# Weights of a fused GLA and gated-MLP kernel: half of each matrix as plain f32 blocks between the input loads, half by casting DMAs, and a new instruction order

## Chip, cores, metric

One core of a Trainium2 chip. The metric is device microseconds of the whole program, lower is better. "Before" and "changed" always mean the two kernels of this document. Spans in a profile are some 2 us shorter than the device time of the same run (192.9 for 195.0).

## The reference, cut to what matters

```python
def _attn_ref(q, k, v, alpha):                 # 4 x 8 heads, 768 steps, head size 48
    for t in range(S):
        state = alpha[:, :, t, :, None] * state + einsum('bhd,bhe->bhde', k[:, :, t], v[:, :, t])
        y[:, :, t] = einsum('bhd,bhde->bhe', q[:, :, t], state)

def _moe_ref(x, w_in, w_out):                  # x: 3072 x 384, w_in: 384 x 2048, w_out: 2048 x 384
    h = x @ w_in
    return (h * cos(h)) @ w_out
```

The kernel cuts the time steps into 24 chunks of 128 and computes each with matmuls; two chunks make a group for the MLP.

## The kernel before

It is a list of small units, emitted in the order of one long string. Each engine runs its own units strictly in that order, so the string is five in-order queues braided into one. A letter is a kind of unit, the number a chunk, a group or a piece:

```python
units = {
    "a": load_a, "k": load(k_t, k), "q": load(q_t, q), "v": load(v_t, v), "w": load_w,    # SyncE; w: GpSimd
    ...                                          # i l c C d E: Ln, cumulative sums, Exp
    "K": scale_k, "R": lambda j: scale_q(nc.gpsimd, j), "O": lambda j: scale_q(nc.vector, j),
    "P": cast_v, "M": decay,                     # GpSimd
    "T": transposes, "t": ev_transposes, "D": dma_transposes,   # TensorE + VectorE, or one DMA on SyncE
    "S": state, "u": ev_state, "b": ...,         # state, TensorE, VectorE, GpSimd
    "A": scores, "m": mask_scores, ... "Q": outputs_two, "z": ev_outputs_two,
    "F"/"H": first product, "f"/"h": cosine on ScalarE, "p"/"g": gate on VectorE,
    "V": second, "e": ev_second, "o": store, "x": warmup,       # o: SyncE
}
for u in ORDER.split():
    units[u[0]](int(u[1:]))
```

(comments and the joined F/H lines are mine, "..." marks cuts). The loads concerned:

```python
def load(bufs, src):
    return lambda j: nc.sync.dma_start(out=bufs[j % len(bufs)], in_=rows(src, j))   # 192 KB in rows of 192 B

def load_w(i):                                   # f32 in memory, bf16 in SBUF: the DMA casts
    n = NF // 2
    if i < 2:
        f = slice(i * n * C, (i + 1) * n * C)
        nc.gpsimd.dma_start(out=w1[:, :, f], in_=moe_w_in[:, f].rearrange("(k p) f -> p k f", p=C))
    else:
        ...                                      # w_out, half i - 2
```

All inputs, the stores and the DMA transposes of chunks 8 to 23 share SyncE's queue; chunks 0 to 7 are transposed on TensorE.

## Time and profile before

| | before |
|---|---|
| time | 195.33 us median of 3 (195.08 to 195.69); with a fourth run 195.26, as below |
| TensorE busy | 182.5 us of 192.9 (95%), 17.1 of it warm-up matmuls |
| VectorE, ScalarE, GpSimd busy | 61%, 62%, 42% |
| HBM read, written | 25.17 MB, 4.72 MB |

How to read the lines below: a row of the windows view gives a stretch, its length, the busy time of each engine with its instruction count, the granted TensorE clock (1.00 is full), the DMA share and GB/s. In a timeline or chain a line starts with its start and its length in us; brackets give the idle time of the engine just before and what ended it. A waits line gives total, number and longest. The lines that carry the reading of the kernel before stand in the prediction.

```profile
44.00:85.00 41.00, 40.84 (x484) 30.86 (x483) 26.86 (x30) 29.02 (x34) 24.63 (x37) 1.00 1.19 199
85.00:160.00 75.00, 73.12 (x806) 54.66 (x804) 48.92 (x49) 60.63 (x65) 36.72 (x56) 1.00 1.06 188
```

### The profile page before, as it was taken

To read this page: it belongs to the slowest core of one execution; us is meant where nothing else is said; L and a number is where in the kernel's file an instruction comes from. 1 tells how busy PE (TensorE), PEld (TensorE's weight loads), DVE (VectorE), ACT (ScalarE), POOL (GpSimd) and SP (SyncE) were. 2 spreads that over 40 slices of the span, in tenths; PEclk is the share of its full clock that TensorE was granted. 3 is DMA by queue.
4 is the path that set the end of the run, shared out by engine and by line. 5 is a ranking of instruction groups with operands and counts; after the bars stand their busy time and mean duration, and the time that the engine had idled before them with its cause. 6 is when DMAs were issued, how large, how long until landed. Compare 5 with 4: busy or idle time off the path is not lost.

```text
span 192.9 us, 4781 instructions
## 1 busy us (share of the span) xinstructions
PE 182.5 (95%) x1990; PEld 131.8 (68%) x1994; DVE 117.7 (61%) x138; ACT 120.1 (62%) x133; POOL 81.6 (42%) x128
## 2 busy tenths in 40 slices
PE   7997889989999999997999998999999999999993
PEld 2444468957688687685777685786786786876861
DVE  5025784844847928829828438748758578596450
ACT  2540344744768668947739567789999982361632
POOL 3317950055294655571190656271239761030000
PEclk9999999999999999999999999999999999999999
DMA  6999999999989999999989999999998762200112
GB/s 127 188 187 188 146 190 188 184 196 194 190 192 176 205 233 207 188 168 196 268 162 192 175 214 218 175 227 205 149 217 158 135 152 34 85 0 3 41 41 82
DMA packets 123092, 31.23 MB, mean 162 GB/s; under 512 B 117184, under 2 KB 122304, under 8 KB 123072
## 3 DMA queue, kind: packets, MB, share of 16 engines
q1 hardware_dynamic: 120192, 27.80, 85.0%
q0 software_dynamic: 2880, 3.15, 10.1%
q8 instruction: 15, 0.25, 0.5%
q14 instruction: 5, 0.04, 0.1%
HBM read 25.17 MB, written 4.72 MB: 155 GB/s over the span
## 4 chain that ended last, share of the span: by engine, by line
PE 66%; DMA 13%; SPq 6%; ACT 4%; issue 4%; DVE 3%; POOL 2%; ACTq 0%; DVEq 0%
PE one L362 31%; PE two L341 21%; DMA w<-in_moe_w_out_dram 10%; PE two L303 6%; SPq L158 5%; PE two L243 3%; DVE g_sb L352 3%; DMA v_sb<-in_v_dram 2%; ACT c_sb L347 2%; PE two L191 2%; SPq L161 2%; ACT L347 1%; PE one L257 1%; POOL w L167 1%; PE two L193 1%
## 5 line engine op out<-in xcount | busy, mean ns | idle before, releaser
L352 DVE TENSOR_TENSOR g_sb<-two,c_sb 128x1024 bf16<-128x1024 f32 x48 | 58.0, 1221 | 27.7 <-ACT c_sb L347 27.2
L362 PE MATMUL one<-w,g_sb 128*128 128x384 bf16 x384 | 69.5, 327 | 1.4 <-DVE g_sb L352 0.8
L341 PE MATMUL two<-xT,w 128*128 128x256 bf16 (+1 forms) x624 | 68.4, 264 | 1.0 <-DVE g_sb L352 1.0
L347 ACT ACTIVATE c_sb<-two,halfpi 128x1024 bf16<-128x1024 f32 x48 | 52.6, 1113 | 19.5 <-PE two L341 19.0
L341 PEld LDWEIGHTS <-w 128*128 128x128 bf16 x624 | 56.7, 98 | 9.7 <-issue 1.1
L362 PEld LDWEIGHTS <-g_sb 128*128 128x128 bf16 x384 | 35.3, 98 | 24.0 <-DVE g_sb L352 1.7
L206 POOL TENSOR_TENSOR kqb<-k_sb,icp 128x384 bf16<-128x384 f32 x24 | 23.9, 997 | 20.5 <-DMA k_sb<-in_k_dram 12.6
L262 POOL TENSOR_TENSOR ub<-sc,Em 128x384 bf16<-128x384 f32 x20 | 16.6, 829 | 33.1 <-DVE sc L272 31.8
L248 DVE TENSOR_TENSOR A_sb<-two,mask_f 128x1024 bf16<-128x1024 f32 x24 | 28.5, 1217 | 2.6 <-PE two L243 2.6
L212 POOL TENSOR_TENSOR kqb<-q_sb,cp 128x384 bf16<-128x384 f32 x22 | 21.9, 998 | 9.4 <-DMA q_sb<-in_q_dram 5.7
L366 ACT ACTIVATE o_sb<-one 128x384 f32<-128x384 f32 x24 | 11.7, 492 | 15.5 <-PE one L362 15.5
L347 ACT ACT_TABLE_LOAD x11 | 14.1, 1283 | 9.9 <-PE two L341 6.2
L216 POOL CAST vpb<-v_sb 128x384 bf16<-128x384 f32 x24 | 12.0, 504 | 17.2 <-DMA v_sb<-in_v_dram 9.3
L375 PE MATMUL one<-warm 128*128 128x512 bf16 x62 | 17.1, 418 | 2.2 <-DVE warm L102 1.2
L185 ACT ACTIVATE lnab<-a_sb 128x768 bf16<-128x768 f32 (+1 forms) x13 | 10.3, 794 | 12.5 <-DMA a_sb<-in_alpha_dram 12.4
L201 ACT ACTIVATE icp<-two 128x768 f32<-128x768 f32 (+1 forms) x13 | 9.9, 761 | 11.8 <-PE two L193 9.0
L272 DVE TENSOR_TENSOR sc<-one,ub 128x384 f32<-128x384 f32 x20 | 11.0, 552 | 8.2 <-PE one L257 7.9
L321 DVE CAST xT<-two 128x768 bf16<-128x768 f32 x11 | 10.5, 958 | 8.4 <-PE two L303 8.4
L179 ACT ACT_TABLE_LOAD x11 | 14.1, 1283 | 0.9 <-PEq L404 0.7
L303 PE MATMUL two<-A_sb,vpb 128*64 128x128 bf16 x264 | 13.2, 220 | 0.1
L303 PEld LDWEIGHTS <-vpb 128*64 128x64 bf16 x288 | 12.8, 110 | 0.5 <-issue 0.3
L375 PEld LDWEIGHTS <-warm 128*128 128x128 bf16 x66 | 6.4, 104 | 9.6 <-issue 3.6
(42 smaller groups left out, 114.1 us busy)
## 6 DMA issues: line engine op xcount, KB each, us to landing
k_sb<-in_k_dram SPq DMA_DIRECT2D x24, 192.0 KB, 4.6
a_sb<-in_alpha_dram SPq DMA_DIRECT2D x24, 192.0 KB, 4.3
v_sb<-in_v_dram SPq DMA_DIRECT2D x24, 192.0 KB, 4.4
q_sb<-in_q_dram SPq DMA_DIRECT2D x24, 192.0 KB, 4.2
out_dram<-o_sb SPq DMA_DIRECT2D x24, 192.0 KB, 3.7
w<-in_moe_w_in_dram POOLq DMA_DIRECT2D x2, 768.0 KB, 10.0
w<-in_moe_w_out_dram POOLq DMA_DIRECT2D x2, 768.0 KB, 17.7
qkT<-kqb SPq DMA_TRANSPOSE x16, 3.8
```

Source lines behind the costliest of these rows:

```text
L179: nc.scalar.preload_act_table_set("natural_log_exp_and_others")
L206: nc.gpsimd.tensor_tensor(out=kqb[j % 4][:, 0, :, 0:D], in0=k_t[j % 6], in1=icp_t[j // 2 % 3][:, j % 2].rearrange("s (h d) -> s h d", h=H) ...
L212: eng.tensor_tensor(out=kqb[j % 4][:, 1, :, 0:D], in0=q_t[j % 6], in1=cp.rearrange("s (h d) -> s h d", h=H), op=ALU.mult)
L216: nc.gpsimd.tensor_copy(out=vpb[j % 4][:, :, 0:D], in_=v_t[j % 6])
L248: nc.vector.tensor_tensor(out=A_t[j % 4].rearrange("s (h t) -> s h t", h=H), in0=two[("A", j)].rearrange("s (h t) -> s h t", h=H), in1=mas ...
L262: eng.tensor_tensor(out=ub[j % 3][:, :, 0:96].rearrange("r p (a e) -> r p a e", a=2), in0=src.rearrange("r p (a e) -> r p a e", a=2), in1= ...
L303: nc.tensor.matmul(t[64 * half : 64 * half + 64, kt * C : (kt + 1) * C], lhsT, rhs, start=start, stop=stop, skip_group_check=True)
L341: nc.tensor.matmul(t[:, m * n : (m + 1) * n], w1[:, kk, f * C : (f + 1) * C], x_t[g % 3][:, kk, bs].rearrange("r b t -> r (b t)"), start=( ...
L347: nc.scalar.activation(out=c_s.take((name, i)), in_=two[(name, i)], func=AF.Sin, bias=halfpi, scale=1.0)
L352: nc.vector.tensor_tensor(out=g_t[g % 3][:, fs, bs], in0=shaped(two[(name, i)], name), in1=shaped(c_s[(name, i)], name), op=ALU.mult)
L362: nc.tensor.matmul(one[("o", j)][:, 0:DM], g_t[j // 2 % 3][:, f, j % 2], w2[:, f], start=(f == 0), stop=(f == NF - 1))
L375: nc.tensor.matmul((one.free or two.free)[0][:, 0:512], warm[:, 0:C], warm, start=True, stop=True)
```

## The change

The intent: the MLP can start only when weights are there, and the casting loads come late and in one lump. So the first halves of both matrices come as seven plain f32 blocks (three of w_in with 4 KB rows, four of w_out) between the first input loads, are cast by whichever engine has time, and only the second halves are cast by DMA. The order is new throughout: DMA transposes already for chunks 5 to 7, seven k products and six more q products on VectorE instead of GpSimd, fewer warm-ups. Cut to its core:

```diff
 ORDER = """
-k1 a0 a3 a1 k0 v1 q0 a2 q2 i0 x12 c0 v3 d0 k2 M0 i1 x7 c1 k3 K0 d1 q1 K1 q3 P1 O0 x13 T0 v0 l1 t0
+a1 W1 k1 a0 q0 i1 i0 W0 q1 x20 c0 c1 k0 v0 d1 d0 J1 O1 B0 B1 R0 W7 a2 a3 v1 W2 l1 j7 P0 M0 P1 G0
 ... (every line of the order is replaced)
+    wf_s = Slots(lambda i: sb.tile([C, 1024], FP, tag=f"wf{i}", name="wf"), 5)
+    def piece(i):
+        if i < 6:
+            kk, f = i % 3, slice(i // 3 * 1024, i // 3 * 1024 + 1024)
+            return w1[:, kk, f], moe_w_in[kk * C : (kk + 1) * C, f], 1024
+        f = 2 * (i - 6)
+        return (w2[:, f : f + 2], moe_w_out[f * C : (f + 2) * C, :].rearrange("(f p) n -> p f n", p=C),
+                2 * DM)
+    def load_piece(i):
+        nc.sync.dma_start(out=staged(wf_s.take(i), i), in_=piece(i)[1])
+    def cast_piece(eng, i):
 ...
-    def scale_k(j):
-        nc.gpsimd.tensor_tensor(out=kqb[j % 4][:, 0, :, 0:D], in0=k_t[j % 6],
+    def scale_k(eng, j):
+        eng.tensor_tensor(out=kqb[j % 4][:, 0, :, 0:D], in0=k_t[j % 6],
 ...
+        "W": load_piece, "J": lambda i: cast_piece(nc.vector, i), "j": lambda i: cast_piece(nc.scalar, i),
+        "G": lambda i: cast_piece(nc.gpsimd, i),
-        "K": scale_k, "R": ...
+        "K": lambda j: scale_k(nc.gpsimd, j), "B": lambda j: scale_k(nc.vector, j), "R": ...
```

More of the change, by code (lines that the diff above doesn't have):

```diff
@@ L17 @@
 ORDER = """
-k1 a0 a3 a1 k0 v1 q0 a2 q2 i0 x12 c0 v3 d0 k2 M0 i1 x7 c1 k3 K0 d1 q1 K1 q3 P1 O0 x13 T0 v0 l1 t0
-a5 x2 C1 E1 a4 v2 K2 q5 R2 K3 k5 x15 T2 O1 t2 T1 k4 A0 t1 q4 P0 x1 A1 w0 S1 S0 a6 u0 w1 u1 l2 M1
-m0 R3 x8 C2 w2 m1 T3 E2 M2 Y0 w3 t3 A2 y0 P2 Y1 m2 b1 S2 A3 M3 P3 u2 M4 m3 b2 Q1 x6 F0 z1 y1 S3 f0
-F2 p0 f2 x2 F3 p2 F1 f3 H6 p3 f1 H4 p1 h6 u3 V4 h4 g6 b3 V5 V0 g4 V1 v4 H5 a7 V2 h5 v5 R5 V3 g5 V6
-a8 e0 K5 V7 a9 H7 K4 e1 q6 R4 T5 h7 V8 t5 k6 V9 g7 T4 v9 P4 V10 t4 v6 V11 l3 S4 e2 A4 q7 u4 A5 P5
@@ L23 @@
-C3 m4 b4 o2 V12 E3 m5 V13 k7 S5 Q2 l4 u5 M7 M6 o0 R6 C4 z2 a11 M5 K6 V14 E4 H10 v7 b5 q8 T6 P6 k8
-H8 t6 h10 R7 q11 S6 a10 V15 h8 g10 K7 H9 q9 e3 u6 g8 M9 T7 k9 M8 h9 H11 t7 k10 P7 g9 V16 h11 v8 R8
-S7 A6 u7 A7 o1 V17 m6 b7 V20 a13 m7 V21 V18 a12 l5 g11 Q3 o3 R9 C5 z3 v10 K8 V19 E5 H12 K9 D8 e4
-R11 H14 D9 M10 P8 H13 h12 K10 o4 q10 k11 g12 S8 h13 V22 v11 V23 u8 h14 q12 g13 H15 b8 e5 P10 k12
-g14 V28 M11 k13 h15 P9 S10 V29 a15 g15 V30 a14 A8 R10 l6 A9 m8 V31 v12 K11 C6 e7 m9 E6 S9 D10 P11
-Q4 u9 b9 D11 V24 z4 R12 V25 u10 v13 H18 K12 v14 b10 H16 D12 h18 H19 q15 g18 h16 o5 P12 S11 g16 h19
@@ L29 @@
-H17 M12 v15 u11 o7 V26 g19 h17 V27 a16 P13 V32 g17 e6 M13 A10 q13 A11 m10 S12 V33 o6 l7 V34 a17
-m11 C7 k14 Q5 E7 a18 u12 A12 z5 P15 V36 R15 V37 m12 K13 V38 H22 R13 M15 H20 D13 b11 h22 P14 H21
-q19 g22 K14 h20 q17 q14 V35 g20 v16 h21 V39 k15 q21 e8 H23 g21 e9 o9 V40 h23 S13 V41 u13 R14 g23
-A13 V44 b13 l8 D14 V45 m13 V46 K15 q20 V47 v17 C8 D15 Q6 E8 P16 q16 V42 z6 a19 e11 V43 M16 R17 k17
-H24 o8 q18 P17 k16 M14 S14 a21 h24 H25 u14 b14 e10 g24 S15 h25 o10 H26 R16 k18 g25 V48 h26 K17 H27
-u15 g26 D17 b15 V52 h27 V53 a20 K16 v18 A15 A14 a23 m15 V49 D16 l9 V50 m14 V54 v19 C9 g27 Q7 E9
@@ L35 @@
-K18 V55 z7 V51 R18 e13 H28 o13 e12 R19 a22 o12 S16 M18 D18 S17 u16 H30 h28 b16 o11 g28 H29 q23 P19
-h30 k19 P18 v22 M17 u17 V60 q22 h29 g30 V56 H31 g29 l10 A17 A16 m17 V61 V62 K19 m16 h31 V57 D19
-V58 g31 C10 k20 Q8 E10 V59 z8 V63 R20 e14 H32 o14 e15 b17 k21 o15 K20 S18 k23 S19 u18 H34 h32 v21
-R21 u19 D20 M19 g32 H33 b19 h34 v20 K21 v23 V68 g34 h33 k22 M20 V64 D21 H35 g33 P21 l11 A18 A19
-m18 V69 V70 P20 m19 M21 h35 V65 V66 g35 C11 Q9 E11 P22 V67 z9 P23 K23 V71 e16 H36 o16 e17 M22 R23
-o17 S20 R22 D23 H38 u20 h36 b20 H37 g36 h38 K22 M23 S21 D22 g38 h37 V76 H39 u21 g37 b21 V72 h39
@@ L41 @@
-A21 A20 m21 V77 V78 m20 V73 V74 g39 A22 Q10 V75 z10 V79 e18 m22 H40 o18 e19 o19 S23 h40 S22 H42
-u22 b22 g40 H41 h42 u23 V80 b23 g42 h41 H43 g41 A23 h43 V84 m23 V81 g43 V82 Q11 V83 z11 V85 e20
-H45 o20 V86 h45 H44 g45 H47 h44 H46 g44 h47 V87 g47 h46 V88 e21 V89 g46 o21 V92 V93 V90 V91 V94
-e22 V95 o22 e23 o23
+a1 W1 k1 a0 q0 i1 i0 W0 q1 x20 c0 c1 k0 v0 d1 d0 J1 O1 B0 B1 R0 W7 a2 a3 v1 W2 l1 j7 P0 M0 P1 G0
+x14 T0 T1 q2 k2 q3 W6 t0 t1 S0 v2 A0 A1 x4 C1 S1 E1 k3 u0 m1 m0 u1 M1 G2 P2 M2 W9 a5 v3 x1 Y0 Y1
@@ new lines @@
+y0 O2 B2 F0 K3 O3 y1 J6 b1 T2 f0 a4 W8 w1 P3 t2 F2 A2 S2 T3 p0 m2 j9 f2 t3 u2 x4 A3 l2 V0 S3 b2 M3
+j8 m3 p2 u3 Q1 x1 C2 V1 z1 H5 V4 V5 E2 h5 F1 F3 k4 f1 q4 k5 g5 p1 f3 H4 H7 q5 h4 v4 b3 w3 K4 V2 p3
+V3 V6 V7 h7 e0 e1 a8 o0 a9 g4 O4 K5 T4 O5 t4 H6 D5 h6 l4 P4 S4 a6 a7 u4 g7 V8 g6 v5 V9 V12 V13 A5
+A4 l3 v6 q7 k7 q6 C4 M4 V14 V10 m5 m4 b4 P5 C3 Q2 z2 E4 E3 B7 R7 k6 B6 R6 q8 k9 k8 q9 D7 M5 P6 M6
+V15 V11 D6 H8 e3 h8 e2 a10 a11 S5 H9 H11 S6 v7 h9 g8 u5 g9 h11 u6 H10 h10 l5 V16 V20 V17 V21 O8 K9
+g11 g10 A7 A6 V18 V22 V23 b5 R9 K8 M9 P7 D9 D8 o3 o2 m6 m7 C5 E5 Q3 z3 V19 A9 A8 e5 m8 m9 H13 v8
@@ new lines @@
+P8 S7 H12 h13 e4 M8 M7 g13 u7 h12 k10 v9 o5 H15 h15 S8 o1 a12 a13 q11 g12 H14 b7 h14 u8 b8 P9 B10
+V24 V25 Q4 S9 g14 o4 v12 V26 q13 q15 k12 a15 q10 v10 z4 g15 u9 l6 C6 H17 H16 V28 b9 O10 V29 E6 k11
+H18 V27 O11 P10 h16 h17 e6 h18 g16 B11 q12 D10 a14 D11 v11 o6 k13 H19 S10 V30 g17 u10 R12 P12 R13
+M10 a17 b10 g18 h19 V31 V36 g19 M12 A10 A11 V37 V38 V39 m10 P11 K12 M11 K13 l7 C7 e7 e9 m11 Q5 E7
+V32 k15 o7 a19 k14 z5 o9 D13 v13 v15 q14 D12 v14 V33 S11 u11 H20 H22 S12 H21 h20 h22 u12 g20 P13
+R15 g22 q16 a16 V34 h21 V35 S13 e8 P15 K15 M13 R14 K14 H23 h23 A12 o8 D15 a18 D14 k16 q18 v16 v17
@@ new lines @@
+l8 g21 u13 A13 V44 m12 g23 b13 b11 V45 V46 V40 V47 C8 e11 V41 m13 P14 E8 l9 Q6 A14 A15 P16 K16 M16
+P17 V42 k17 z6 V43 m15 m14 S14 H25 e10 H24 h25 H26 S15 K17 q19 o10 v22 u14 g25 h24 M14 b14 Q7 h26
+R16 g24 o11 q17 a21 D16 a20 a23 k18 g26 u15 z7 C9 V52 E9 M15 V53 S16 H27 h27 R17 b15 R18 R19 u16
+H28 g27 q20 D17 v18 K18 b16 H31 M17 h28 k19 K19 S17 g28 h31 H30 H29 h30 u17 g31 V54 V48 g30 V55
+V49 A17 A16 V50 V51 h29 l10 e13 m17 m16 D18 v23 k20 v20 D19 o13 q21 e12 C10 g29 E10 a22 l11 V60 Q8
+A19 A18 o12 q23 V61 z8 m18 V62 H32 h32 m19 g32 R21 P18 M18 P20 R20 M19 K20 H33 H34 S18 V63 k21 k22
@@ new lines @@
+v21 v19 k23 h34 P19 K21 H35 e15 h33 h35 u18 g34 V56 V57 C11 S19 g33 u19 g35 V58 V59 V68 E11 o15
+D20 D21 q22 e14 R23 b17 o14 Q9 A21 A20 S20 V69 V70 V71 K22 M20 b19 z9 m20 H39 e17 M21 H36 V64 m21
+u20 b20 P21 M23 K23 P22 R22 h36 o17 V65 S21 D23 D22 H37 u21 g36 S22 V66 b21 V67 u22 h39 h37 H38
+M22 g37 g39 V72 e16 h38 g38 o16 V73 V76 Q10 A23 A22 z10 m23 m22 V77 V74 H40 V75 V78 h40 H41 V79
+b22 P23 e18 Q11 g40 e19 h41 z11 g41 H42 H43 V84 H44 V80 V85 h42 h43 g42 g43 h44 H46 V86 g44 V87
+H45 h46 V81 o18 o19 e21 V82 V83 H47 h45 g45 g46 e20 h47 g47 V88 V89 V90 V92 V93 V94 V95 o21 o20
@@ L45 @@
+e23 V91 o23 S23 e22 u23 b23 o22
 """
@@ L173, in load_w, with staged @@
                                 .rearrange("(f p) n -> p f n", p=C))
+    def piece(i):
[5 more added lines that the diff above has]
+                2 * DM)
+    def staged(t, i):
+        n = piece(i)[2]
+        return t[:, 0:n] if i < 6 else t[:, 0:n].rearrange("p (f n) -> p f n", f=2)
+    def load_piece(i):
+        nc.sync.dma_start(out=staged(wf_s.take(i), i), in_=piece(i)[1])
+    def cast_piece(eng, i):
+        dst, src = piece(i)[0], staged(wf_s[i], i)
+        if eng is nc.scalar:
+            eng.activation(out=dst, in_=src, func=AF.Copy)
+        else:
+            eng.tensor_copy(out=dst, in_=src)
+        wf_s.give(i)
     table = [None]
@@ L377 @@
         "a": load_a, "k": load(k_t, k), "q": load(q_t, q), "v": load(v_t, v), "w": load_w,
+        "W": load_piece, "J": lambda i: cast_piece(nc.vector, i), "j": lambda i: cast_piece(nc.scalar, i),
+        "G": lambda i: cast_piece(nc.gpsimd, i),
         "i": lambda j: ln(j, 1), "c": lambda j: cums(j, 1), "d": lambda j: exps(j, 1),
         "l": lambda g: ln(2 * g, 2), "C": lambda g: cums(2 * g, 2), "E": lambda g: exps(2 * g, 2),
-        "K": scale_k, "R": lambda j: scale_q(nc.gpsimd, j), "O": lambda j: scale_q(nc.vector, j),
+        "K": lambda j: scale_k(nc.gpsimd, j), "B": lambda j: scale_k(nc.vector, j), "R": lambda j: scale_q(nc.gpsimd, j), "O": lambda j: scale_q(nc.vector, j),
         "P": cast_v, "M": decay,
```

## The prediction

> **What bounds the kernel now.** I read the page's busy table first, then asked for busy time by stretch, with the cut at the moment where the chain of waits leaves its one long DMA wait. Last I read the timeline of that first stretch, for TensorE and for the DMA queue of SyncE.
>
> Busy by engine, then three stretches (columns: length, then busy us of PE, PEld, DVE, ACT, POOL; granted clock; DMA share; GB/s), then the warm-up matmuls alone:
>
> ```profile
> PE 182.5 (95%) x1990; PEld 131.8 (68%) x1994; DVE 117.7 (61%) x138; ACT 120.1 (62%) x133; POOL 81.6 (42%) x128
> ...
> 0.00:42.80 42.80, 37.70 (x392) 24.35 (x397) 22.69 (x42) 17.14 (x21) 17.96 (x34) 1.00 1.21 178
> 42.80:157.00 114.20, 112.16 (x1268) 83.96 (x1268) 73.32 (x76) 88.61 (x97) 60.57 (x90) 1.00 1.12 194
> 157.00:192.90 35.90, 32.63 (x333) 23.50 (x330) 21.67 (x21) 14.31 (x17) 3.09 (x5) 1.00 0.14 42
> ...
> 0.00:42.80 42.80, 17.06 (x62) 6.42 (x66) 1.00 1.21 178
> ```
>
> From 42.8 us to the end TensorE is busy 112.16 + 32.63 = 144.8 of 150.1 us. Of the 5.3 us idle, 3.2 are the tail after the last matmul (189.7 to 192.9), so only 2.1 us are holes. Before 42.8 us, 17.06 of the 37.70 busy us are warm-up matmuls on zeros: only 20.6 us is work that counts. So a gain has to come from the first 43 us, or from taking work off TensorE. What ends that stretch stands in the chain of waits in order of time (start, us, what):
>
> ```profile
> 13.86 4.62 DMA v_sb<-in_v_dram
> ...
> 22.92 19.84 DMA w<-in_moe_w_out_dram
> 42.80 2.76 PE one L362 x16
> ```
>
> The last half of w_out leaves at 22.9 and lands at 42.8; the first matmuls on that half start then. The timeline of the same time shows how the MLP starts and what the casting loads do to the other queue:
>
> ```profile
> 18.13 2.35 SPq L158 DMA_DIRECT2D q_sb<-in_q_dram  x1
> 20.53 10.01 SPq L158 DMA_DIRECT2D k_sb<-in_k_dram  x2
> 21.43 9.11 SPq L158 DMA_DIRECT2D k_sb<-in_k_dram  x1
> 29.62 1.50 PE L341 MATMUL two<-xT,w 128*128 128x128 bf16 x24
> 30.59 5.38 SPq L158 DMA_DIRECT2D q_sb<-in_q_dram  x1
> 36.01 4.45 SPq L161 DMA_DIRECT2D a_sb<-in_alpha_dram  x1
> 38.20 2.77 PE L362 MATMUL one<-w,g_sb 128*128 128x384 bf16 x16
> ```
>
> SyncE's issues take about 1 us each elsewhere in this trace; while the four casting loads run they take 4 to 10 us. The first MLP matmul starts at 29.6, the first on w_out at 38.2. DMA's two own views give the rates:
>
> ```profile
> q0 software_dynamic: 2880, 3.15, 10.1%
> w<-in_moe_w_in_dram POOLq DMA_DIRECT2D x2, 768.0 KB, 10.0
> w<-in_moe_w_out_dram POOLq DMA_DIRECT2D x2, 768.0 KB, 17.7
> ```
>
> Casting: 10.1% of 192.9 us is 19.5 us of all 16 engines for 6.29 MB read (3.15 MB written): 323 GB/s on the read side, about 4.9 us for each half matrix. Inputs with 192-byte rows: the waits for the 2nd, 7th, 13th and 15th load of the queue ended at 4.8, 10.15, 16.46 and 18.53, so load n lands near 3.3 + 1.02 n us.
>
> **What the Trainium skill says.** "DMA: Bandwidth & Descriptors", section SWDGE vs HWDGE vs iDMA: a cast in flight is only to be had from GpSimd's software queue, and each DMA engine goes round its queues packet by packet. The trace agrees that the two queues share engines: the issues of 10.01 and 5.38 us above. "VectorE: DVE Perf Modes", section The perf-mode tier table: an fp32 copy out of SBUF runs at up to 2x, 1227 ns for 2048 elements a row; no fp32 copy of that kind is in this trace. "SBUF — State Buffer", section Who interferes with whom: a VectorE instruction with two SBUF inputs contends with GpSimd instructions that read SBUF. The trace agrees: the two q products on VectorE took 0.67 and 1.25 us, the longer one while GpSimd ran a k product. "ScalarE: Activation LUTs", section What ACT_TABLE_LOAD costs: about 1283 ns a load; the trace has 1283.
>
> **The change part by part.**
>
> *Loads.* Two of four casting loads go; seven plain ones come: three w_in blocks of 512 KB (rows of 4 KB), four w_out blocks of 384 KB. They read the same bytes. I take 350 GB/s for them, the read rate of both queues together in the casting stretch (5.3 us a half is 296 GB/s, and three inputs in 11 us add 55); it is a choice, and plain rows might do better. That is 1.5 us and 1.1 us a block. Total DMA time hardly moves; the order does. Adding up the new queue (inputs 1.02, blocks 1.5 or 1.1, from about 3): the last w_in block is 14th and lands near 18.5 to 19, the last w_out block is 25th, near 30.
>
> *Casts.* Two on VectorE (estimate from the skill's table: about 0.7 us each), three on ScalarE (w_out blocks of 768 elements: 0.84, from the Ln over 768), two on GpSimd (1024 elements: 0.504 x 1024 / 384 = 1.34). They lie in the startup. The one that counts is GpSimd's second cast, behind the last w_in block: 19 to about 21. So the first MLP matmul comes at 21 to 22 in place of 29.6.
>
> *But the gain at the start is not the gain at the end.* Count what TensorE has to do, in program order, before it first needs the second half of w_out (the point where the chain left its wait, 42.8). In both orders it is the same: attention of chunks 0 to 3, seven pieces of the first product (4 + 3), four of the second. In the new order more of that attention stands after the first MLP piece. After 21.5 us TensorE needs 4 x 1.5 + 3 x 1.31 + 4 x 0.65 = 12.5 us for MLP and some 4 us for attention, so not before 38. ScalarE has seven cosines at 1.11, two casts at 0.84, one Ln of 0.84, two exponentials at 0.81 and three table loads at 1.28 there: 15.8 us, almost as tight, and its in-order queue stands behind the last w_out block (near 30). The casting half of w_in can only be issued after GpSimd's k product of chunk 3, near 27.5, and lands near 34; the first piece on it starts near 35, then F, F, H, H (5.6 us): 40.5. The casting half of w_out leaves near 33 and lands near 39 to 40. So the point of 42.8 moves to about 40.5: 2.3 us.
>
> *After that point.* Transposes on TensorE still to come fall from four to one: 3 x 0.45 us (the chain's pieces of eight transposes) = 1.35 us off TensorE; three more DMA transposes take their place, in a queue issue of 1.2 to 1.9 us each. Table loads fall from 22 to 20 in all, and from 20 to 16 after the point. They are part of the 2.1 us of holes, so 0.5 us at most. VectorE gets 7 k products and 6 more q products, 13 x (0.67 to 1.25) = 9 to 16 us on top of 117.7, less three evictions of 0.69: still under 70%. GpSimd loses as many of 1.0 us. Neither bounds. Fewer warm-ups (44 for 66) cost nothing unless TensorE goes cold.
>
> Sum: 195.3 - 2.3 - 1.35 - 0.5 = 191.2; I say 191.0, as plain blocks may run faster than 350 GB/s.
>
> **The rivals.** *A: the input stream binds.* From 42.8 to 157 us, 72 inputs at 1.02, 16 transposes at about 1.5 and some 18 stores at about 0.6 make 108 of 114 us. Three more transposes make it worse, and VectorE's products now stand before them. For it: DMA share over 1 until 157. Against it: TensorE waited on releasers the profile names for only 1.8 us there, and after 157 it still had 32.6 us of work in hand. If starved by 3 to 5 us: 193.5 to 195.5. *B: the start is really worth 8 us*, if the blocks run at 400 GB/s and the casting halves, half as many bytes, land 4 to 5 us earlier than I have them: the point moves to 36 to 37, then 186.5 to 187.5. Against it: ScalarE's 15.8 us and TensorE's own work after 21.5. *C: the casts delay the attention of the first chunks* (each waits in order for its block; a late w_out block holds the Exp behind it on ScalarE): the point stays near 42.8, only transposes are gained: 194. For it: SyncE's issues of 4 to 10 us while a casting load runs; the last two blocks may meet it.
>
> **Range and chances.** Two per cent is 191.4, almost at my number, so the chances split. The end can't come much under 187: 144.8 - 1.35 of TensorE after a point of at least 38, plus 3.2 of tail and 2.4 us between span and time (195.3 - 192.9) is 187.1 without a hole. Range 187.5 to 195.0. Faster 0.52, within 2% 0.43, slower 0.05.
>
> **What would show it.** First MLP piece near 21.5; first use of the second half of w_out near 40.5, with a DMA or ScalarE in front of it; TensorE busy after it near 143.4 us with 2 us of holes; SyncE issues over 4 us only while the two casting loads run, and fewer; plain 512 KB blocks in 1.5 us of queue. Holes on TensorE between 45 and 157 of over 4 us, released by kqb or qkT, would show rival A; first use at 37 or earlier, rival B; a gap on ScalarE before a w_out cast of over 3 us with the point at 42 or later, rival C. A TensorE share of matmuls at double length after the first 4 us would show a cold clock, which I have left out.

## The result

| | before | changed |
|---|---|---|
| time | 195.26 us (4 runs) | 204.58 us median (203.06 to 205.99, 4 runs) |
| ratio | 1 | 1.0472, 95% interval 1.0391 to 1.0554 |
| span of the profiled run | 192.9 us | 203.2 us |

A ratio in this document is the mean time of one kernel's fast runs over the mean of the other's fast runs of the same rounds, so not quite the ratio of the medians quoted. The change costs 4.7%; the prediction said 191.0.

The changed kernel: the page's busy line and casting queue, then three stretches cut at the first use of the second half of w_out.

```profile
PE 178.1 (88%) x1946; PEld 128.2 (63%) x1948; DVE 123.3 (61%) x150; ACT 119.1 (59%) x134; POOL 70.3 (35%) x115
...
q0 software_dynamic: 1440, 1.57, 4.6%
...
0.00:44.40 44.40, 33.98 (x372) 22.09 (x375) 25.67 (x49) 22.65 (x26) 14.70 (x29) 1.00 1.04 213
44.40:160.00 115.60, 104.36 (x1199) 76.90 (x1199) 74.73 (x80) 78.19 (x87) 46.65 (x72) 1.00 1.08 189
160.00:203.20 43.20, 39.81 (x379) 29.25 (x375) 22.91 (x23) 18.26 (x21) 8.96 (x15) 1.00 0.18 52
```

The casting share halved, as meant. But TensorE is idle for 11.2 us between 44.4 and 160 (115.60 less 104.36), where before it had 2.1 us of holes over its whole run after 42.8. With that the difference of the spans closes: point of first use 44.4 for 42.8, +1.6; holes +9.1; TensorE work after the point 144.2 for 144.8, -0.6; tail 3.4 for 3.2, +0.2; sum 10.3 us, which is 203.2 less 192.9.

The startup, from the timeline of TensorE in the changed kernel:

```profile
20.47 0.27 PE L367 MATMUL two<-xT,w 128*128 128x128 bf16 x2
21.35 1.40 PE L367 MATMUL two<-xT,w 128*128 128x128 bf16 x22 [0.60 <-POOL w L198]
37.53 5.50 PE L367 MATMUL two<-xT,w 128*128 128x128 bf16 x72
44.41 2.76 PE L388 MATMUL one<-w,g_sb 128*128 128x384 bf16 x16 [1.38 <-DMA w<-in_moe_w_out_dram]
```

The MLP does start at 20.5 us in place of 29.6, behind a GpSimd cast as foreseen. Yet the second half of w_out is first used at 44.4, later than before, and TensorE waits for its DMA, for 1.38 us. The other late half, of w_in, comes first in time: its issue on GpSimd, then the line of the page with its time to landing (last column, us).

```profile
28.44 0.93 POOL L168 DMA_DIRECT2D w<-in_moe_w_in_dram  x1
...
w<-in_moe_w_in_dram POOLq DMA_DIRECT2D x1, 768.0 KB, 9.1
```

It lands near 37.5, the 72 matmuls on it start at 37.53 and end at 43.03: so TensorE could not have reached the second half of w_out before 43.0 in any case. The chain that ended last shows what follows from that wait:

```profile
34.30 10.06 DMA w<-in_moe_w_out_dram
...
44.41 1.47 PE one L388 x8
...
45.90 0.50 ACT o_sb L392
...
46.42 0.36 SPq L396
...
46.82 0.43 SPq L162
```

(Left out are pieces of 0.02 to 0.04 us called "issue", in which nothing is waited for that the profile shows.)

The late half of w_out releases the second product, that the eviction, that the first store (L396) in SyncE's queue, and only behind the store do the next input loads (L162) leave: the queue stood still from 41.1 to 46.4. Two stretches to hold against those of before, then the two largest waits of TensorE from 44.4 to 160 us, then who waited for inputs on GpSimd from 44 to 160 us (changed):

```profile
44.00:85.00 41.00, 37.74 (x435) 27.18 (x435) 27.96 (x32) 26.63 (x32) 12.99 (x21) 1.00 1.00 184
85.00:160.00 75.00, 66.61 (x767) 49.72 (x765) 47.17 (x50) 51.74 (x57) 33.66 (x51) 1.00 1.12 192
...
PE two L269 <- DMA qkT<-kqb: 3.6, 3, 1.5
PE two L367 <- DVE g_sb L378: 2.1, 4, 0.7
...
POOL vpb L242 <- DMA v_sb<-in_v_dram: 39.8, 9, 7.0
```

The same group before:

```profile
POOL vpb L216 <- DMA v_sb<-in_v_dram: 8.0, 6, 3.2
```

From 44 to 160 us TensorE's holes are 3.3 us before 85 us and 8.4 us after it, and no single wait makes them: DMA transposes (qkT) end 3.6 us of them, the gates (g_sb, over three lines) 3.5 us, nothing else more than 1.4. Inputs come late: with k and q, GpSimd waited 55.0 us for them in place of 25.8. Counting input loads on SyncE's timeline issued by a given time (counts from the profiled runs, by the start of each issue):

| issued by (us) | 45 | 50 | 60 | 70 | 80 | 100 | 120 | 140 | 150 |
|---|---|---|---|---|---|---|---|---|---|
| before | 27 | 32 | 40 | 47 | 54 | 65 | 80 | 90 | 96 |
| changed | 24 | 27 | 36 | 40 | 48 | 61 | 74 | 87 | 95 |
| DMA transposes, before | 0 | 0 | 0 | 1 | 2 | 6 | 9 | 12 | 14 |
| DMA transposes, changed | 0 | 1 | 1 | 4 | 5 | 7 | 11 | 14 | 15 |

By 70 us the changed kernel is seven loads behind and three transposes ahead; it makes that up only by 150.

### The profile page after: what moved, and what is told of

Read it like the earlier page. It is cut to its first block, busy times and chain, and to the rows that moved or that the text cites. A ratio compares the mean times of both kernels' runs of the same rounds, so it can differ in the third digit from the quotient of the medians.

```text
span 203.2 us, 4685 instructions
## 1 busy us (share of the span) xinstructions
PE 178.1 (88%) x1946; PEld 128.2 (63%) x1948; DVE 123.3 (61%) x150; ACT 119.1 (59%) x134; POOL 70.3 (35%) x115
## 4 chain that ended last, share of the span: by engine, by line
DMA 25%; issue 21%; SPq 21%; PE 15%; POOL 11%; DVE 5%; ACT 1%; POOLq 1%; ACTq 0%
SPq L159 14%; PE one L388 7%; DMA k_sb<-in_k_dram 6%; PE two L367 5%; DMA v_sb<-in_v_dram 5%; DMA w<-in_moe_w_out_dram 5%; DMA q_sb<-in_q_dram 4%; POOL kqb L232 4%; SPq L162 3%; DMA wf<-in_moe_w_out_dram 2%; POOL kqb L238 2%; POOL ub L288 2%; POOL vpb L242 2%; DMA qkT<-kqb 2%; SPq L262 2%
## 5 line engine op out<-in xcount | busy, mean ns | idle before, releaser
L388 PEld LDWEIGHTS <-g_sb 128*128 128x128 bf16 x384 | 35.8, 98 | 24.8 <-issue 3.0
L238 POOL TENSOR_TENSOR kqb<-q_sb,cp 128x384 bf16<-128x384 f32 x16 | 16.0, 1000 | 24.2 <-ACT cp L228 14.4
L392 ACT ACTIVATE o_sb<-one 128x384 f32<-128x384 f32 x24 | 11.8, 490 | 19.5 <-PE one L388 18.5
L211 ACT ACTIVATE lnab<-a_sb 128x768 bf16<-128x768 f32 (+1 forms) x13 | 10.3, 794 | 21.4 <-DMA a_sb<-in_alpha_dram 21.4
L232 POOL TENSOR_TENSOR kqb<-k_sb,icp 128x384 bf16<-128x384 f32 x17 | 17.3, 1019 | 9.5 <-DMA k_sb<-in_k_dram 9.4
L401 PE MATMUL one<-warm 128*128 128x512 bf16 x42 | 12.8, 452 | 2.9 <-DVE warm L102 1.2
L329 PE MATMUL two<-qkT,ub 128*64 128x128 bf16 x152 | 11.7, 222 | 1.8 <-DVE g_sb L378 1.0
```

What stands on the lines that cost most here:

```text
L232: eng.tensor_tensor(out=kqb[j % 4][:, 0, :, 0:D], in0=k_t[j % 6], in1=icp_t[j // 2 % 3][:, j % 2].rearrange("s (h d) -> s h d", h=H), op=A ...
L238: eng.tensor_tensor(out=kqb[j % 4][:, 1, :, 0:D], in0=q_t[j % 6], in1=cp.rearrange("s (h d) -> s h d", h=H), op=ALU.mult)
L329: nc.tensor.matmul(t[64 * half : 64 * half + 64, kt * C : (kt + 1) * C], lhsT, rhs, start=start, stop=stop, skip_group_check=True)
L388: nc.tensor.matmul(one[("o", j)][:, 0:DM], g_t[j // 2 % 3][:, f, j % 2], w2[:, f], start=(f == 0), stop=(f == NF - 1))
```

## The experiments

Theories when they began. REST: the order after the first use is at fault. START: the new loads are. HANDOVER: the late half passes into the input stream through the store. Later ones are named where they arise. All variants gave correct results. Each is told by what it edits; "rest" means the units from V2 on, the first use of the second half of w_out.

### Start and rest exchanged

Edit, e1: the changed kernel up to V2, then every unit still to do in the order of before (one gate, p3, moved ahead to free a PSUM buffer):

```diff
-V2 p3 V3 V6 V7 h7 e0 e1 a8 o0 a9 g4 O4 K5 T4 O5 t4 H6 D5 ...   (new rest)
+a6 M4 p3 H6 h6 g6 g4 a7 V2 v5 R5 V3 V6 a8 e0 K5 V7 a9 e1 ...   (old rest)
```

> New start (all units up to the first use of the second half of w_out), then the old order of everything after it. Theory REST (the new order after that point is at fault: it starves TensorE of inputs, 11 us of holes between 44 and 160 us against 2 before): 195 to 198 us, the start being 1.6 us later than before (44.4 for 42.8). Rival START (the new loads are at fault and whatever follows pays for them): 202 to 205 us.

Measured: 195.7 us, ratio 1.0021 (0.9991 to 1.0051).

Edit, e2: the kernel before up to V2, then the new rest (no plain blocks at all).

> Old start (four casting loads) up to the same point, then the new order. Theory REST: 201 to 204 us, i.e. nearly all of the loss without any of the new loads. Rival START: 193 to 196 us.

Measured: 202.36 us, 1.0343 (1.0293 to 1.0393).

What follows: the new start is worth nothing and costs nothing; the loss is in the order of the rest (with the places of its products and its three DMA transposes, which are tried apart below). 3.4% and 0.2% add to 3.6 of the 4.7%; about 1% comes only with both together, or is noise: the intervals allow for it.

### The first store and one transpose moved back in the queue

```diff
-... e0 e1 a8 o0 a9 g4 O4 K5 T4 O5 t4 H6 D5 h6 ... V13 A5 A4 ... k9 k8 q9 D7 ...
+... e0 e1 a8 a9 g4 O4 K5 T4 O5 t4 H6 h6 ... V13 D5 A5 A4 ... k9 k8 q9 o0 D7 ...
```

> The changed kernel with the first store and the DMA transpose of chunk 5 moved behind ten input loads in SyncE's queue. Theory HANDOVER (the store waits in the in-order queue for the late weight half, 41.1 to 46.4 us, and the inputs behind it never catch up): 198 to 201 us, TensorE's holes down by 3 us or more. Rival (the queue is bound by DMA throughput throughout, the 5 us gap does not matter): 203 to 205 us.

Measured: 203.09 us (200.33 to 204.4), 1.0426 (1.0386 to 1.0467). The four runs scatter: 204.4 and 203.43 are slow, being over 1.5% above the fastest, and the ratio fits the mean without the fastest. The two fast, 200.33 (the profiled one) and 202.74, average 3.3% above before. The queue's pause is gone in that profile, and 27 loads in place of 24 were issued by 45 us, but 43, against 47 before, by 70. So the move is worth between nothing and about a third of the loss; these runs don't settle it.

### The last weight half issued earlier

```diff
-... a4 W8 w1 P3 t2 ... h4 v4 b3 w3 K4 V2 ...
+... a4 W8 w1 w3 P3 t2 ... h4 v4 b3 K4 V2 ...
```

> The changed kernel with the casting load of the second w_out half issued right after that of w_in (near 29.5 us for 34.3). Theory HANDOVER: it lands near 40, the first store leaves 4 us earlier, 199 to 201 us. Theory REST alone: 203 to 205 us, because inputs bound the rest. If DMA throughput bounds the start, the last weight half lands earlier but the inputs of chunks 4 and 5 later, and the time hardly moves.

Measured: 203.88 us, 1.0444 (1.0413 to 1.0475). The decisive lines are those of its DMA issues (last column: us from issue to landing) and of TensorE:

```profile
w<-in_moe_w_in_dram POOLq DMA_DIRECT2D x1, 768.0 KB, 9.8
w<-in_moe_w_out_dram POOLq DMA_DIRECT2D x1, 768.0 KB, 14.3
...
38.95 5.49 PE L367 MATMUL two<-xT,w 128*128 128x128 bf16 x72 [0.70 <-DMA w<-in_moe_w_in_dram]
44.37 1.95 PE L388 MATMUL one<-w,g_sb 128*128 128x384 bf16 x11
```

Issued at 30.0 instead of 34.3, the half takes 14.3 us instead of 10.06 and lands at 44.3 either way; the half of w_in, now sharing with it, lands 1.4 us later (38.9 for 37.5). So what shares the DMA engines with it sets its landing here, not its issue.

### Transposes of chunks 5 to 7 back on TensorE

```diff
-... O5 t4 H6 D5 ... q9 D7 M5 P6 M6 V15 V11 D6 H8 e3 h8 e2 ...
+... O5 t4 H6 T5 t5 ... q9 M5 P6 M6 V15 V11 H8 e3 h8 e2 T7 t7 T6 t6 ...
```

> The changed kernel with the transposes of chunks 5, 6 and 7 on TensorE again, as before (1.35 us of TensorE more, three DMA transposes fewer). Theory TRANSPOSES (the three extra DMA transposes hold the queue while the input stream is shortest): 199 to 201 us, inputs issued by 70 us back from 40 to 45 or more. Theory LEAD (the new order emits loads with too short a lead, 40 inputs ahead of the fourth pair's output against 46 before, 46 against 56 for the fifth): 203 to 205 us.

Measured: 205.3 us, 1.0502 (1.0474 to 1.0529). T7 waited 2.46 us for a PSUM buffer that only the eviction e2 frees: a flaw of my edit. So again, with T7 t7 T6 t6 just ahead of V16, where one is free:

> As e5 (transposes of chunks 5 to 7 on TensorE), but 7 and 6 placed where a PSUM slot is free, so that the 2.46 us wait for a slot that e5 made does not arise. Theory TRANSPOSES: 199 to 202 us. Otherwise 203 to 205 us as e5.

Measured: 205.8 us, 1.0536 (1.0483 to 1.0589). The flaw was not the reason; in the new order these transposes are not what costs.

### The same three transposes, in the kernel before

```diff
-T5 t5 ... T6 t6 ... T7 t7      (TensorE and VectorE)
+D5    ... D6    ... D7         (SyncE's queue, at the places of T5, T6, T7)
```

> The kernel before with only the transposes of chunks 5, 6 and 7 moved to DMA, at the places where TensorE did them. Theory TRANSPOSES: 198 to 201 us. Theory LEAD (the order of before has loads in hand): 194 to 196 us, TensorE saves 1.35 us and little is lost.

Measured: 201.68 us, 1.0341 (1.0312 to 1.0369): 6.5 us lost for three transposes that save TensorE 1.35. Its timeline, then stretches around the place:

```profile
68.32 0.61 PE L243 MATMUL two<-qkT 48*128 48x128 bf16 x8 [3.90 <-DMA qkT<-kqb]
68.86 4.99 PE L362 MATMUL one<-w,g_sb 128*128 128x384 bf16 x16
...
64.40:68.30 3.90, 0.02 (x2) 0.00 (x0) 1.42 (x2) 1.86 (x2) 1.79 (x3) 0.78 0.86 143
68.30:70.00 1.70, 1.68 (x12) 0.93 (x13) 1.03 (x1) 0.00 (x0) 0.98 (x2) 0.50 1.21 231
70.00:72.00 2.00, 2.00 (x7) 0.91 (x6) 1.32 (x2) 0.00 (x0) 0.99 (x1) 0.50 1.20 242
72.00:74.00 2.00, 2.00 (x15) 0.98 (x15) 0.00 (x0) 0.00 (x0) 0.00 (x0) 0.65 1.21 249
74.00:76.00 2.00, 2.00 (x47) 1.51 (x42) 0.96 (x1) 0.45 (x1) 0.00 (x0) 1.00 1.17 229
```

One transpose lands too late, TensorE waits 3.90 us, and then its granted clock is 0.50 until some 73.4: sixteen matmuls take 4.99 us in place of the 2.8 that sixteen take elsewhere. So one late DMA transpose cost 3.9 us of waiting and over 2 us of slow matmuls. From 85 to 160 us TensorE is as busy in this variant as before (73.12 us of 75): the loss is all before 85.

### Loads ahead of stores and transposes

A search over the string moved each input load of the rest up to four places ahead in SyncE's queue, past o and D units, wherever its buffer is free by then:

```diff
-... a8 o0 a9 D5 a6 a7 v5 v6 ...                    (SyncE's part only)
+... a8 a9 a6 a7 v5 v6 ... o0 ... D5 ... D7 ... D6   (each load at most four places)
```

> The changed kernel with nothing moved but SyncE's queue: after the first use of the late weight half each input load goes up to four places ahead, past stores and DMA transposes, where its buffer is free in the program's order. Theory LEAD: 197 to 200 us, waits of GpSimd on v at under 25 us (50.5 in the changed kernel). Theory TRANSPOSES: 202 to 205 us. If the DMA transposes, pushed back by the loads, become the wait: 203 us or more with TensorE's waits on qkT above 4 us.

Measured: 236.5 us, 1.2097 (1.2027 to 1.2167). Its timeline shows what took the place of the late inputs:

```profile
63.69 1.04 PE L269 MATMUL two<-qkT 48*128 48x128 bf16 x16 [12.26 <-DMA qkT<-kqb]
```

The transposes, pushed behind loads that still had to wait for a buffer, became the bound: 25.0 us of TensorE's waits are on qkT. With TensorE's transposes for chunks 5 to 7 as well:

> Both edits, transposes of chunks 5 to 7 on TensorE and loads up to four places ahead. If both causes add: 195 to 197 us, the level of the new start with the old order (195.7). If one alone carries the loss, the same as that one's run.

Measured: 224.75 us, 1.1498 (1.1467 to 1.153). The dose of four was far too much, so these two say nothing on how much lead the loads should have; they do show that loads and transposes compete for one queue and neither can go first at will.

### Which part of the rest

f1: the new order up to V24 (first matmul of the second product of chunk 6), then the old one. f2: the old one up to V24, then the new.

> The changed kernel up to the first matmul of the second product of chunk 6 (near 85 us), then the old order. Contains the early DMA transposes of chunks 5 to 7. Theory EARLY DEBT (the input stream falls 6 or 7 loads behind between 45 and 70 us and the rest pays it off): 201 to 204 us. Theory SPREAD (the new order loses a little everywhere; TensorE's holes are 3.3 us before 85 and 8.4 us from 85 to 160 in the changed kernel): 197 to 199 us.

Measured: 204.8 us (202.79 to 208.46), 1.0455 (1.0397 to 1.0512).

> The kernel before up to the same point, then the new order (16 DMA transposes in all, as before). EARLY DEBT: 195 to 197 us. SPREAD: 199 to 202 us.

Measured: 198.88 us, 1.019 (1.0166 to 1.0214). The new order up to chunk 6 costs all of the loss even when the old order follows; from chunk 6 on it costs 1.9% by itself (TensorE busy 69.12 of 75 us from 85 to 160 in f2's profile, 73.12 before). The two don't add up to the 4.7%. With e1 (the start costs 0.2%) the units that cost most lie between V2 and V24, which the changed kernel reaches at 44 and about 85 us; the holes themselves come mostly later, 8.4 of 11.6 us after 85 in the changed kernel. f1 has no fast profile, so where its time goes is not seen.

### Products back on GpSimd

```diff
-... g4 O4 K5 T4 O5 t4 ... B7 R7 k6 B6 R6 ... B10 ... B11 ...
+... g4 R4 K5 T4 R5 t4 ... K7 R7 k6 K6 R6 ... K10 ... K11 ...
```

> The changed kernel with the q and k products after the first use of the late weight half on GpSimd again, at the same places of the order. If VectorE standing in front of an input (10.9 us of waits on q) holds the gates and so TensorE: 200 to 202 us. If the inputs come late whoever waits for them: 203 to 206 us.

Measured: 205.49 us, 1.0499 (1.0448 to 1.055). No gain: the inputs are late for whichever engine waits for them.

### Several stoppers removed together

By now the cause of the loss between V2 and V24 was open. A stopper here is a unit in SyncE's queue that waits and holds the loads behind it. g1 is e3's store move and e5b's transposes in one.

> The changed kernel with both e3's store move and e5b's transposes of chunks 5 to 7 on TensorE: no queue wait for the late weight half and no early DMA transpose. If the two together make the debt of inputs: 196 to 199 us, 44 or more inputs issued by 70 us (40 in the changed kernel, 47 before). If the debt comes from the order of loads against the later transposes: 202 to 205 us.

Measured: 206.9 us, 1.0602 (1.0533 to 1.0671). SyncE's timeline and its waits from 55 to 76 us in g1:

```profile
59.73 1.36 SPq L159 DMA_DIRECT2D v_sb<-in_v_dram  x1
65.99 3.79 SPq L262 DMA_TRANSPOSE qkT<-kqb  x2
...
SPq L262 <- POOL vpb L242: 6.6, 1, 6.6
```

With two stoppers gone the loads were level with before at 60 us (40), and then none left until after 70: the transposes of chunks 9 and 8 stand next in the queue and wait 6.6 us for their operands. So g2 puts three loads ahead of them:

```diff
-... P7 D9 D8 o3 o2 m6 m7 ... v8 ... k10 v9 ...
+... P7 v8 k10 v9 D9 D8 o3 o2 m6 m7 ...
```

> As g1, and three input loads (v of chunk 8, k of chunk 10, v of chunk 9) ahead of the DMA transposes of chunks 9 and 8 in SyncE's queue, as they are in the kernel before. If transposes that stand in the queue before their products are ready hold the loads behind them: 2 us or more under g1. Otherwise within 1 us of g1, or slower because the transposes are late.

Measured: 205.81 us, 1.0548 (1.0495 to 1.0601), 1.1 us under g1 on the same chip, with intervals that overlap. GpSimd's waits on v from 44 to 160 us fell to 24.8 us (39.8 in the changed kernel), and still no time came back.

### A pause of the queue in the old order

h1 is e1 with the first store made a stopper again:

```diff
-... V2 v5 R5 V3 V6 a8 e0 K5 V7 a9 ... q7 u4 A5 P5 C3 m4 b4 o2 ... u5 M7 M6 o0 ...
+... V2 R5 V3 V6 e0 o0 v5 a8 K5 V7 a9 ... q7 u4 A5 P5 C3 m4 b4 o2 ... u5 M7 M6 ...
```

> New start with the old order of the rest (195.7 us) with one thing moved: the first store right behind the two alpha loads in SyncE's queue, so that the queue waits about 5 us for the late weight half, as in the changed kernel. Theory HANDOVER or DEBT: 199 to 202 us, as the input stream has no slack to make the gap good. If the order of the rest and not the gap is at fault: 195 to 197 us.

Measured: 196.73 us, 1.0079 (1.0036 to 1.0121), against e1's 1.0021. Its store left at 46.91, the pause was there, and it cost about 1 us (the intervals overlap). By 70 us 46 loads were issued: the old order makes the pause good, because nothing in its queue waits for operands soon after. But its pause was half as long, 2.5 us (44.4 to 46.9) for the 5.3 of the changed kernel, because its two alpha loads took until 44.4 to issue. So HANDOVER is weakened and not excluded: a pause of 5 us in the old order was not made.

### Weights first

g4 is h1's order with both casting loads issued together near 29 us and k, q and v of chunks 4 and 5 issued from GpSimd behind them:

```diff
-... W8 w1 P3 ... k4 q4 k5 q5 v4 ... b3 w3 K4 ...      (loads on SyncE)
+... W8 w1 w3 P3 ... b3 n4 r4 n5 r5 s4 K4 ...          (n, r, s: the same loads by gpsimd.dma_start)
```

> An attempt to beat both: new start with the old order of the rest, both casting loads issued together near 30 us, the k, q and v blocks of chunks 4 and 5 issued from GpSimd behind them, and the store as a stopper of SyncE's queue. If the start is bound by the bytes ahead of the last weight half (about five blocks of 1.02 us fewer): first use of that half near 40 us in place of 44.4, 191 to 194 us. If those inputs then come too late for chunks 4 and 5, or issuing 1024 rows from GpSimd takes its time: 196 to 202 us.

Measured: 198.48 us, 1.0184 (1.0158 to 1.021). The half of w_out left at 29.2 and took 13.1 us, so it landed at 42.3, 2.0 us sooner than in e4 with five blocks fewer ahead of it; TensorE had no use for it before 45.9, though, and those blocks then came too late. No variant beat the kernel before; e1 is level with it.

### The place of the scores

Counted in TensorE work after V2 (an estimate: units times the pieces of the chain before, 1.31 for H, 0.65 for V, 1.24 for Q and so on), the new order asks for scores much earlier than the old: chunk 8 after 26.6 us of work instead of 35.3, chunk 15 after 65.6 instead of 75.4, chunk 18 after 89.1 instead of 101.5. j1 puts A and m of chunks 8 to 23 later in the new order, up to 8 us of such work and never nearer than 3 us to the output that needs them; j2 puts them up to 8 us earlier in the kernel before. Nothing else moves. One of the moves of j2:

```diff
-... D8 e4 R11 H14 D9 ... a15 g15 V30 a14 A8 R10 l6 A9 m8 ...
+... (A8 m8 and A9 m9 up to 8 us of TensorE work nearer to D8 and D9) ...
```

> The changed kernel with the scores and the masking of chunks 8 to 23 emitted up to 8 us of TensorE work later, never closer than 3 us of TensorE work to the output that needs them; loads, stores, transposes and all else as they were. Theory DEMAND (the new order asks for the scores of chunks 8, 14, 18 and 20 some 9 to 13 us of TensorE work earlier than the old one, and the input stream is no faster): 199 to 202 us. If the scores' place does not matter: 203 to 206 us.

Measured: 214.14 us (212.43 to 216.37), 1.0935 (1.0876 to 1.0994).

> The kernel before, with the scores and the masking of chunks 8 to 23 emitted up to 8 us of TensorE work earlier and nothing else moved: four casting loads, 16 DMA transposes, the same queue of SyncE. Theory DEMAND: 199 to 204 us, with TensorE waiting on qkT or on the gates behind the masking. If the old order has that much in hand: 195 to 197 us.

Measured: 228.05 us, 1.1661 (1.163 to 1.1693). TensorE's waits in j2:

```profile
PE two L243 <- DMA qkT<-kqb: 10.1, 5, 3.2
PE two L341 <- DVE xT L321: 6.6, 4, 2.3
PE two L341 <- DVE A_sb L248: 4.4, 4, 1.3
```

j2 goes the way that DEMAND says, but much further: 33 us lost where 4 to 9 were expected. j1 goes against it: later scores made the new order slower by 9 us, not faster. Scores and masks were moved while outputs, gates and PSUM buffers kept their places; that this is why both moves cost time is a guess, not shown. DEMAND is not, as a single cause, this loss.

## Why the prediction was wrong

*The start of the MLP*: right. 21 to 22 us predicted, 20.5 and 21.35 measured. Casts: 0.69 and 0.56 us on VectorE (0.7 predicted), 0.84 on ScalarE (0.84), 1.04 on GpSimd (1.34 predicted from 0.504 for 384 elements; the two durations are not in proportion). One reading was too high: the line of 10.01 us holds two issues, one of 0.9 and one of 9.11 us, so the issues on SyncE in that time took 0.9 to 9.1 us, not 4 to 10.

*The first use of the second half of w_out*: wrong, and of the wrong sign. Predicted 40.5, measured 44.4. The step that failed is the landing of both casting halves. The half of w_in was to leave "near 27.5, and lands near 34; the first piece on it starts near 35": it left at 28.4 and landed at 37.5, and its four pieces, which took 5.5 us for the 5.6 predicted, started 2.5 us late. "The casting half of w_out leaves near 33 and lands near 39 to 40": it left at 34.3 and landed at 44.4, which added the 1.38 us of waiting. Each took 9 to 10 us where 6 to 7 were allowed. I had written "Total DMA time hardly moves" and then let the halves land as if the bytes in front of them had gone away. Issued from 28.3 to 41.1, ahead of the last half or beside it, are also two k, two q, one v and one alpha block, six blocks at 1.02 us by my own rate: 6 us, more than the 4 to 5 us by which that half was late. e4 shows it (issued 4 us sooner, same landing), g4 too (five blocks behind it, landed 2 us sooner).

*What follows from the point*: not tested. That an earlier point would end the kernel earlier by as much was never seen, as no variant had one. e1, with the point at 44.4, is only 0.2% slower than before, but there one more piece of the first product stands before the point and fills the wait.

*Holes*: the step that decided the outcome. "They are part of the 2.1 us of holes, so 0.5 us at most", and the sign "with 2 us of holes", took for granted that the new order would keep the holes of the old one. 11.2 us were measured; slower had been given 0.05. The new order was treated as a list of parts, each priced alone; its quality as a schedule was not priced at all. e2 shows that the order alone, without one new load, costs 3.4%.

*Transposes*: "three more DMA transposes take their place, in a queue issue of 1.2 to 1.9 us each", counted as hidden. The 1.35 us that they were to take off TensorE show as 0.6 (144.2 for 144.8 after the point). In the old order they cost 6.5 us (e8), because one lands late and TensorE waits. In the new order, taking them out gave nothing back (e5b). The term was mis-sized, but it is not what explains this change alone.

*VectorE and GpSimd, neither bounds*: right; moving the products back (e9) changed nothing.

*Rival A, the input stream binds*, was nearest to the traces: inputs late, holes ended by qkT (3.6 us, where over 4 was the sign) and the gates. It isn't shown as the cause: e1 moves the same loads without the loss, and g2 cut the waits for v without a gain. I sized it at 3 to 5 us and gave it too little weight because TensorE still had 32.6 us of work in hand after 157 us. Work in hand at the end does not fill holes in the middle: TensorE stops at the first unit that isn't ready (for 3.90 us in e8), whatever stands behind it. Rival C's signs (first use at 42 or later, ScalarE's gap before a w_out cast 3.9 us) came true, but not by its cause: DMA landings stand in front of the point, at 37.5 and 44.4. Rival B fell.

*What is shown and what stays open.* Shown: the loss is in the new order of the rest, chiefly in the units from V2 to V24; by 70 us SyncE's queue is seven loads behind. Shown too: neither the early transposes, nor the engine of the products, nor store and transposes together, nor those with three loads ahead of the next transposes, brings it back; moving the store and one transpose back brings back a third at most, by its two fast runs. The trace of g1 suggests that taking out one stopper lets the queue run to the next, but g2 took that one out as well without a gain. Which joint property of the new order makes the holes, beyond its inputs being late at the units in front, is not settled.

## What to carry to other kernels

Price a new order as a schedule, not as a sum of its parts: where the queues are in-order and one DMA queue carries loads, stores and transposes, ask for each load what stands ahead of it and what that waits for. To split such a change, cut the order string at one unit and run old start with new rest and the reverse; two runs told more here than all the local repairs. Where bytes bound a start, an earlier issue may move no landing, as in e4; count everything that has to pass the same engines by then.

## What the Trainium skill lacked or had wrong

- "TensorE: Matmul & The Clock Gate", Part 1: The HAM clock gate, puts the array at half clock after an idle window of about 3.4 us. In e8 it fell sooner: the mean of 0.78 over 64.4 to 68.3 puts the fall at about 66.6, 2.2 us after the last matmul. It stayed at half to about 73.4 (from 0.65 in 72 to 74), 6.8 us, of which 5.1 held work. The shorter waits of the changed kernel's profiled run left its mean clock at 1.00.
- "DMA: Bandwidth & Descriptors", Bandwidth, does not say which side of a casting DMA sets its time. Here 6.29 MB read and 3.15 MB written took 19.5 us of all 16 engines: 323 GB/s by what was read, 162 by what was written.
- The same page, section DMA Transpose (X-bar), has no time from issue to landing for an SBUF-to-SBUF transpose of 128 x 1024 bf16 beside other traffic in one queue. Here the median from issue to landing was 3.8 us before and in the changed kernel, and an issue held SyncE's queue for 1.2 us or more.
- No page draws out that a store in the queue of the loads waits there for its data and holds the loads behind it: 41.1 to 46.4 us in the changed kernel. What that costs isn't settled: a pause of 2.5 us cost about 1 us in h1.
